# A gated MLP behind linear attention: the spatial product of two of four batches by Strassen's scheme, and another written order

## Chip, cores and metric

One core of one Trainium2 chip runs the whole program. The metric is device time in microseconds (us) of one execution, lower is better. TensorE, VectorE, ScalarE, GpSimd and the queue of SyncE, which issues the DMAs, each run their own list of instructions in the order in which the program wrote them, and wait for one another by semaphores. In rows and code they are PE, DVE, ACT, POOL and SP; PEld is the load of TensorE's stationary operand.

## What is computed

Linear attention with a forget gate comes first, 4 batches of 8 heads, 768 steps, 48 wide; its output, 768 by 384 for each batch, goes into a gated MLP that mixes along the sequence.

```python
f = 1.0 / (1.0 + np.exp(-f_logit))
for t in range(S):
    state = f[:, :, t, :, None] * state + np.einsum('bhd,bhe->bhde', k[:, :, t], v[:, :, t])
    y[:, :, t] = np.einsum('bhd,bhde->bhe', q[:, :, t], state)
...
h = np.maximum(x @ w_in, 0.0)
u, v = (h[..., :d_ff // 2], h[..., d_ff // 2:])
v_n = (v - mu) / np.sqrt(var + 1e-06)
v_s = np.einsum('ts,bsd->btd', w_spatial, v_n) + b_spatial[None, :, None]
gated = u * v_s
return (gated @ w_out)
```

The spatial product is `w_spatial` (768 by 768) times `v_n` (768 by 512), once for each batch.

## The kernel before

**The work is a list of named steps.** `PLAN` (lines 44 to 109) is a table of step names with their arguments; the program calls `step_<name>` for each in turn, and so the table alone sets the order on every engine. A name in `BESIDES` (lines 112 to 119) takes the step's other form: for `sm`, `ys`, `r2` and `c` it says which of two engines does it, for `V`, `U` and `S` it swaps the second and third pass. `Slots` hands out buffers: a step takes one, and it is free again when its last user calls `done`.

**Attention** runs over 24 tiles of 128 tokens (n, six for each batch). The steps `LF`, `LK`, `LQ` load; `c`, `e`, `z`, `h`, `g`, `k`, `q` make the decayed keys and queries; `X`, `YS`, `kv`, `Yq` are its small matmuls in two PSUM pairs `bp`; `w`, `m`, `r0`, `r1`, `r2` stand between them; `ys`, `xt`, `xh`, `xl` copy, transpose and split the tile's output.

**Every large product is done in three passes.** A factor x is held as hi, a copy rounded to the matmul's own type (fp32r), and lo = x - hi; the product is hi·hi + hi·lo + lo·hi, so each 128 by 128 block costs three matmuls. For each of `v`, the gated value and the weights, ScalarE makes hi and VectorE lo.

**The MLP** of batch b, in halves th of 384 tokens:
- `V:b,u` (line 493) makes the v half of h for tile u, 9 matmuls of 512 columns; `vr` is its ReLU, `bs` the moments, `na`, `nb`, `nc` the factor of the norm, `vn` applies it, `vh` and `vl` (lines 562 to 576) split it.
- `U:b,th,c` (line 578) makes u for the block c of 128 channels, 9 matmuls of 384 columns; `ur` is its ReLU.
- `S:b,th,c` (line 592) is the spatial product for 128 channels c and 384 tokens th: 3 passes by 6 blocks of the 768 steps, 18 matmuls of 384 columns in one PSUM bank `mm`. There are 8 such groups for each batch. `sg` (line 606, VectorE) adds the bias and takes the result out of PSUM.
- `sm` multiplies with u, on VectorE or on GpSimd, `sh` and `sl` split, `O:b,th,tt` (line 644) is the output product, 12 matmuls, `oc` copies out and `od` stores.

```python
acc = mm.take(("s", b, th, c))
...
nc.tensor.matmul(
    acc[:, 0:TH], vns.of((b, ks))[va][:, cs], w_sp_s[wb][:, ks, th * TH:(th + 1) * TH],
```

**Buffers.** PSUM has four single banks `mm` and two pairs `bp`. The attention's tiles lie in a pool `attn` on one side of SBUF until the plan ends. At the end of the plan a branch asks whether any gate was too small (`flag`, `check`, `load`), and the last three stores stand behind it.

**The order around the change.** The plan mixes attention and MLP: attention's last tile, `Yq:23`, stands behind all eight `S` of batch 2, and the eight `S` of batch 3 come after attention.

Of the kernel before, what the change touches and what calls it, by code (L numbers as in the profile page):

```python
# [19 lines left out]
T = 128  # L20
# [29 lines left out]
    g:5 LF:7 ct:U,0 c:7 fm:3 w:4 r0:3 m:4 r1:3 r2:3 vr:0,1 xt:2 xh:2 xl:2 ch:U,0 V:0,0 LU:1 YS:4 cl:U,0 LF:6 kv:4  # L50
    h:5 fm:5 fm:4 r0:4 e:7 Yq:3 V:0,2 ys:3 xt:3 LK:5 LQ:5 c:6 e:6 z:6 ca:U,1 r1:4 r2:4 vr:0,0 q:5 LK:6 k:5 ct:U,1
    X:5 g:6 h:6 Yq:4 q:6 U:0,0,0 LF:8 LK:7 vr:0,2 m:5 ys:4 xt:4 nm:0,0 ch:U,1 xh:3 z:7 k:6 c:8 w:5 YS:5 kv:5 cl:U,1
    r1:5 xl:3 X:6 xh:4 xl:4 r0:5 Yq:5 vc:0,1 ys:5 vc:0,2 sq:0,2 h:7 fm:7 q:7 w:6 m:6 g:7 k:7 V:0,3 LQ:6 YS:6 kv:6
    r0:6 e:8 z:8 sq:0,1 vc:0,0 sq:0,0 X:7 w:7 na:0,0 ur:0,0,0 nb:0,0 LF:9 c:9 Yq:6 kj r1:6 xt:5 xh:5 r2:6 m:7 V:0,4
# [36 lines left out]
    sm:2,0,3 g:21 k:21 S:2,1,0 ys:19 od:1,1,0 e:22 xt:19 xh:19 z:22 xl:19 w:20 LF:23 S:2,1,2 YS:20 sg:2,1,0 X:21
# [56 lines left out]
def tile_kernel(ctx, tc, fkq, fn, vv, w_cv, w_spT, b_sp, out):  # L148
# [695 lines left out]
```

## Time and profile before

| | us |
|---|---|
| median of 3 runs | 352.7 (350.92 to 355.41) |
| the profiled execution, its own time | 352.25 |
| its span, first to last instruction | 350.4 |
| outside the span | 1.85 |
| TensorE busy in the span | 334.1 (95%) |
| mean granted TensorE clock | 0.990 of full |

TensorE's busy time counts a matmul until its end leaves the array, so neighbours overlap; what a group of matmuls costs in a run is read from the pieces of the chain of waits, which go from start to start. VectorE's instructions overlap in the same way, by less.

### The profile page before, as it was taken

To read this page: it belongs to the slowest core of one execution; us is meant where nothing else is said; L and a number is where in the kernel's file an instruction comes from. 1 tells how busy PE (TensorE), PEld (TensorE's weight loads), DVE (VectorE), ACT (ScalarE), POOL (GpSimd) and SP (SyncE) were. 2 spreads that over 40 slices of the span, in tenths; PEclk is the share of its full clock that TensorE was granted. 3 is DMA by queue.
4 is the path that set the end of the run, shared out by engine and by line. 5 is a ranking of instruction groups with operands and counts; after the bars stand their busy time and mean duration, and the time that the engine had idled before them with its cause. 6 is when DMAs were issued, how large, how long until landed. Compare 5 with 4: busy or idle time off the path is not lost.

```text
span 350.4 us, 10471 instructions
## 1 busy us (share of the span) xinstructions
PE 334.1 (95%) x4590; PEld 311.7 (89%) x4590; DVE 218.7 (62%) x436; ACT 171.4 (49%) x349; POOL 46.4 (13%) x69
## 2 busy tenths in 40 slices
PE   4689999999999999999999999999999999999993
PEld 3577888989999899999889989999989989999993
DVE  2799879999896966446574675535557657132140
ACT  7776799683645645124544754233443534121231
POOL 3123111303200101003020030012001200001100
PEclk9899999999999999999999999999999999999998
DMA  7849485745323503021630332400101000001012
GB/s 246 331 116 296 153 291 167 281 145 160 91 93 116 204 1 137 2 74 64 178 118 2 125 106 87 159 2 1 47 4 45 4 22 24 22 7 40 23 49 74
DMA packets 14981, 36.01 MB, mean 103 GB/s; under 512 B 1488, under 2 KB 10192, under 8 KB 14928
## 3 DMA queue, kind: packets, MB, share of 16 engines
q1 hardware_dynamic: 14928, 35.26, 30.3%
q8 instruction: 38, 0.62, 0.8%
q14 instruction: 15, 0.12, 0.1%
HBM read 30.54 MB, written 4.72 MB: 101 GB/s over the span
## 4 chain that ended last, share of the span: by engine, by line
PE 89%; DMA 4%; ACT 2%; DVE 1%; issue 1%; SPq 1%; POOL 0%; ACTq 0%; DVEq 0%
PE mm L598 29%; PE mm L636 15%; PE mm L499 14%; PE mm L584 13%; PE bp L385 5%; PE bp L437 4%; PE bp L449 3%; PE bp L409 2%; PE mm L462 2%; DMA fkq<-fkq 2%; DMA words<-w_cv 2%; PE mm L340 2%; POOL fkq L325 0%; DVE fkq L357 0%; SPq L311 0%
## 5 line engine op out<-in xcount | busy, mean ns | idle before, releaser
L607 DVE TENSOR_TENSOR gt<-mm,b_bc 128x384 f32<-128x384 f32 x32 | 17.7, 553 | 37.7 <-PE mm L598 37.7
L598 PE MATMUL mm<-w_sph,vnh 128*128 128x384 f32 x192 | 40.1, 344 | 0.5 <-ACT vr L513 0.5
L598 PE MATMUL mm<-w_spl,vnh 128*128 128x384 f32 x192 | 39.0, 338 | 0.0
L598 PE MATMUL mm<-w_sph,vnl 128*128 128x384 f32 x192 | 39.0, 338 | 0.0
L598 PEld LDWEIGHTS mm<-w_sph,vnh 128*128 128x128 f32 x192 | 33.4, 188 | 0.9 <-ACT vr L513 0.6
L598 PEld LDWEIGHTS mm<-w_spl,vnh 128*128 128x128 f32 x192 | 34.2, 188 | 0.0
L598 PEld LDWEIGHTS mm<-w_sph,vnl 128*128 128x128 f32 x192 | 34.2, 188 | 0.0
L614 POOL TENSOR_TENSOR uT<-gt,uT 128x384 f32<-128x384 f32 x12 | 14.1, 1176 | 149.0 <-DVE gt L607 97.7
L589 ACT ACTIVATE uT<-mm 128x384 f32<-128x384 f32 x32 | 15.5, 489 | 27.4 <-PE mm L584 27.4
L618 ACT CAST gh<-uT 128x384 fp32r<-128x384 f32 x32 | 16.0, 511 | 21.1 <-DVE uT L614 13.4
L622 DVE TENSOR_TENSOR gl<-uT,gh 128x384 fp32r<-128x384 f32 x32 | 17.4, 555 | 13.0 <-ACT gh L618 13.0
L385 PE MATMUL bp<-q,fkq 48*64 48x112 f32 x768 | 23.4, 260 | 0.4 <-DVE fkq L357 0.4
L325 POOL TENSOR_SCALAR fkq<-fkq 112x512 f32<-112x512 f32 (+1 forms) x11 | 16.7, 1515 | 53.4 <-DMA fkq<-fkq 21.7
L584 PE MATMUL mm<-xTh,w_inh 128*128 128x384 f32 x96 | 23.0, 347 | 0.0
L652 ACT COPY osb<-mm 128x384 f32<-128x384 f32 (+1 forms) x25 | 11.4, 465 | 23.6 <-PE mm L636 23.6
L361 DVE TENSOR_TENSOR q<-fkq,F 112x512 f32<-112x512 f32 x24 | 16.4, 684 | 9.6 <-ACT F L346 7.9
L636 PE MATMUL mm<-w_outh,gh 128*128 128x384 f32 (+1 forms) x100 | 22.3, 337 | 0.0
L636 PE MATMUL mm<-w_outh,gl 128*128 128x384 f32 (+1 forms) x100 | 22.1, 333 | 0.0
L584 PE MATMUL mm<-xTh,w_inl 128*128 128x384 f32 x96 | 22.1, 338 | 0.0
L584 PE MATMUL mm<-xTl,w_inh 128*128 128x384 f32 x96 | 22.0, 338 | 0.0
L499 PE MATMUL mm<-w_inh,xTh 128*128 128x512 f32 x72 | 21.8, 410 | 0.0
L636 PE MATMUL mm<-w_outl,gh 128*128 128x384 f32 (+1 forms) x100 | 21.6, 331 | 0.0
(106 smaller groups left out, 704.0 us busy)
## 6 DMA issues: line engine op xcount, KB each, us to landing
fkq<-fkq SPq DMA_DIRECT2D x16, 768.0 KB, 4.6
val<-vv SPq DMA_DIRECT2D x24, 192.0 KB, 4.4
out<-osb SPq DMA_DIRECT2D x24, 192.0 KB, 2.0
fkq<-fkq SPq DMA_DIRECT2D x8, 512.0 KB, 6.0
words<-w_cv SPq DMA_DIRECT2D x4, 768.0 KB, 6.6
fkq<-fn SPq DMA_DIRECT2D x8, 192.0 KB, 3.2
late<-w_cv SPq DMA_DIRECT2D x2, 768.0 KB, 5.7
spat<-w_spT SPq DMA_DIRECT2D x3, 384.0 KB, 5.0
```

Of the source, the lines that this page charges most:

```text
L325: (nc.gpsimd if beside("c", n) else nc.vector).tensor_scalar(f, f, -LOGIT_MOST, None, op0=ALU.max)
L361: nc.vector.tensor_tensor(qs[n % 2][:, :, :, 0:C], *(x.rearrange("p (j c t) -> p j c t", c=T // C, t=C) for x in (parts(n)[2], Fs[n % 2])) ...
L385: nc.tensor.matmul(sc[to, e, cs], k[dr, at:at + C], qs[n % 2][dr, j, chunk], start=True, stop=True)
L499: nc.tensor.matmul(acc, xs[:, c, ut * P:(ut + 1) * P], ws[:, c, G:FF], start=i == 0, stop=i == 3 * KX - 1)
L584: nc.tensor.matmul(acc[:, 0:TH], ws[:, kx, cs], xs[:, kx, :], start=i == 0, stop=i == 3 * KX - 1)
L589: nc.scalar.activation(uTs.take((b, th, c)), mm.of(("u", b, th, c))[:, 0:TH], AF.Relu)
L598: nc.tensor.matmul(acc[:, 0:TH], vns.of((b, ks))[va][:, cs], w_sp_s[wb][:, ks, th * TH:(th + 1) * TH], start=i == 0, stop=i == 3 * KS - 1,)
L607: nc.vector.tensor_tensor(gts.take((b, th, c)), mm.of(("s", b, th, c))[:, 0:TH], b_bc[:, th * TH:(th + 1) * TH], op=ALU.add)
L614: (nc.vector if beside("sm", b, th, c) else nc.gpsimd).tensor_tensor(uT, gts.of((b, th, c)), uT, op=ALU.mult)
L618: nc.scalar.copy(gs.take((b, th, c), HU)[0], uTs.of((b, th, c)))
L622: nc.vector.tensor_tensor(lo, uTs.of((b, th, c)), hi.bitcast(F32), op=ALU.subtract)
L636: nc.tensor.matmul(acc[:, ms], gs.of((b, th, c))[ga][:, ts], w_out_s[wb][:, c, ms], start=c == cs[0] == 0 and ga == wb == 0, stop=c == cs[ ...
```

## The change

Batches 0 and 1 keep the product as it was. For batches 2 and 3 each factor is cut in four, the steps s and the tokens in halves of 384, the channels in halves of 256, and the four block results come from seven block products in place of eight.

- `P:b,k,i` is block product i (1 to 7) for the half k of its 256 channels: 3 passes by 3 blocks, 9 matmuls of 384 columns. A batch has 14 of them. It accumulates in a bank named A, B, D or E; 3, 6 and 7 go on in a bank that has been read out in between.
- `p1`, `p2`, `p3`, `p5`, `c1`, `c3`, `c4`, `c5` are VectorE's additions out of PSUM: 16 for each batch where there were 8 `sg`.
- `xs` makes one of four sums of blocks of v (VectorE, 128 by 384), `ah` and `al` split it: 8 of each for a batch. `vh` and `vl` of the first three tiles are done for 256 of the 512 columns.
- `LY`, `ts`, `th`, `tl`, once: four quarters of the weights are loaded anew, 576 KB each, subtracted (`ts`, VectorE, 128 by 1152) and split into four twin factors (`th` ScalarE, `tl` VectorE). They lie where attention's tiles were; twin 4 takes the place of a quarter of the weights.
- `mst` closes attention's pool and the two PSUM pairs and opens four more single banks, `mn`; `mwin` opens the buffers of the sums, two more `gt` and one more `g`. `mr0` and `mr1` make two tiles of 3 by 512 for v of batches 2 and 3.
- The plan is written anew from the first line to the last: attention ends before the first spatial product of batch 2, `Oa` is not used any more, and `sm`, `c`, `r2` are shared out differently: GpSimd does 13, 8 and 13 of them, where it did 12, 11 and 10.

```diff
 PLAN = """
-    LF:0 constants LF:1 LK:0 kq:0 LF:2 c:0 LQ:0 e:0 kz z:0 kq:1 c:1 e:1 c:2 h:0 q:0 g:0 k:0 LV:1 ca:V,1 ct:V,1 z:1
+    LF:0 constants kz LF:1 kq:1 c:0 e:0 LF:2 kq:0 c:1 LK:0 e:1 z:0 g:0 k:0 h:0 q:0 c:2 kj e:2 LV:1 z:1 LQ:0 ca:V,1
...
-    mm = Slots(tiles(ps, "mm", 4, [P, 512]))
-    bp = Slots(tiles(ps, "bp", 2, [P, 2, 512]))
+    banks = tiles(ps, "mm", 4, [P, 512])
+    mm, bp = Slots(banks), Slots(tiles(pair_pool.enter_context(tc.tile_pool(name="pairs", bufs=1, space=PSUM)), "bp", 2, [P, 2, 512]))
...
+    def step_mst():
+        attn_pool.close()
+        win = win_pool.enter_context(tc.tile_pool(name="win", bufs=1, side="right", reuse_waits="tile"))
+        for i in (1, 2, 3):
+            twin[i] = [win.tile([P, HU, TH], F32R, name=f"T{k}{i}") for k in "hl"]
+        twin[4] = [w[:, 0:HU, TH:S] for w in w_sp_s]
+        made = made_pool.enter_context(tc.tile_pool(name="made", bufs=1, side="right", reuse_waits="tile"))
+        spare.extend(tiles(made, "y", 4, [P, HU, TH]))
+        pair_pool.close()
+        mm.free.extend(tiles(bank_pool.enter_context(tc.tile_pool(name="more", bufs=1, space=PSUM)), "mn", 4, [P, 512]))
+
+    def step_mwin():
+        nonlocal sxs
+        made_pool.close()
+        win = sums_pool.enter_context(tc.tile_pool(name="xsum", bufs=1, side="right", reuse_waits="tile"))
+        sxs = Slots([tuple(win.tile([P, HU, P], F32R, name=f"x{k}{i}") for k in "hl") for i in range(4)])
+        gts.free.extend(tiles(win, "gx", 2, [P, TH]))
+        gs.free.append(tuple(win.tile([P, TH], F32R, name=f"gy{k}") for k in "hl"))
...
-        nc.scalar.activation(vns.take((b, u), 2 * KG)[0], vrs.of((b, u)), AF.Copy, **scaled)
+        cs, uses = direct(b, u), 2 * KG if b not in WIN else 2 if u < HU else 4
+        nc.scalar.activation(vns.take((b, u), uses)[0][:, cs], raw(b, u)[:, cs], AF.Copy, **scaled)
...
+    def step_LY(i):
+        ks, th = {1: (0, 0), 2: (HU, 1), 3: (0, 1), 4: (HU, 0)}[i]
+        src = w_spT[ks * P:(ks + HU) * P, th * TH:(th + 1) * TH]
+        nc.sync.dma_start(spare[i - 1], src.rearrange("(k p) n -> p k n", k=HU))
+
+    def step_ts(i):
+
+        left, right = {1: (3, 1), 3: (2, 3), 2: (2, 1), 4: (4, 2)}[i]
+        nc.vector.tensor_tensor(spare[i - 1], spare[left - 1], spare[right - 1], op=ALU.subtract)
+
+    def step_th(i):
+        nc.scalar.copy(twin[i][0], spare[i - 1])
+
+    def step_tl(i):
+        hi, lo = twin[i]
+        nc.vector.tensor_tensor(lo, spare[i - 1], hi.bitcast(F32), op=ALU.subtract)
+
+    def quarter(b, k, i, j):
+        return raws.of((b, j))[:, :, i * 2 * P + k * P:i * 2 * P + (k + 1) * P]
+
+    SUMS = {1: ((1, 1), (1, 0), (1, 1), ALU.add), 3: ((1, 0), (0, 0), (1, 0), ALU.subtract),
+            2: ((0, 0), (1, 1), (0, 0), ALU.subtract), 4: ((0, 1), (0, 1), (0, 0), ALU.subtract)}
+
+    def step_xs(b, k, i):
+
+        *at, op = SUMS[i]
+        to, x, y = (quarter(b, k, *ij) for ij in at)
+        nc.vector.tensor_tensor(to, x, y, op=op)
+
+    def step_ah(b, k, i):
+        nc.scalar.copy(sxs.take((b, k, i))[0], quarter(b, k, *SUMS[i][0]))
+
+    def step_al(b, k, i):
+        hi, lo = sxs.of((b, k, i))
+        nc.vector.tensor_tensor(lo, quarter(b, k, *SUMS[i][0]), hi.bitcast(F32), op=ALU.subtract)
+        raws.done((b, SUMS[i][0][1]))
...
+    FACTORS = {1: ("A", (0, 0), (0, 0)), 2: ("B", (0, 1), (1, 0)), 3: ("D", 4, (1, 1)), 4: ("E", (1, 1), 4),
+               5: ("D", 1, 1), 6: ("A", 2, 2), 7: ("A", 3, 3)}
+    BANKS = {"A": 4, "B": 1, "D": 2, "E": 1}
+
+    def step_P(b, k, i):
+        name, left, right = FACTORS[i]
+        user = ("P", name, b, k)
+        if i in (1, 2, 4, 5):
+            mm.take(user, BANKS[name])
+        for n, (va, wb) in enumerate(order("P", b, k, i)):
+            for ks in range(HU):
...
+                nc.tensor.matmul(
+                    mm.of(user)[:, 0:TH], x, y, start=n == ks == 0 and i not in (3, 6, 7), stop=n == ks == 2,
+                    skip_group_check=True,
+                )
...
+    def part(name, b, k, th, c, first):
+        acc, at = mm.of(("P", name, b, k))[:, 0:TH], (b, th, c)
+        add = b_bc[:, th * TH:(th + 1) * TH] if first else gts.of(at)
+        nc.vector.tensor_tensor(gts.take(at) if first else add, acc, add, op=ALU.add)
+        mm.done(("P", name, b, k))
+
+    def step_p1(b, k):
+        part("A", b, k, 0, k, True)
...
+    def step_c1(b, k):
+        part("B", b, k, 0, k, False)
```

Three places where the lists of instructions differ.

TensorE, the spatial product of batch 2 before: the last matmul of one group of 18 (`S:2,0,0`) and the first seven of the next. The bank is mm, vnh and vnl are the two parts of v, w_sph and w_spl those of the weights, and the numbers tell buffers apart.

```order
L598 MATMUL mm_130<-w_sph,vnl_154 128x384
L598 MATMUL mm_133<-w_sph,vnh_149 128x384
L598 MATMUL mm_133<-w_sph,vnh_147 128x384
L598 MATMUL mm_133<-w_sph,vnh_145 128x384
L598 MATMUL mm_133<-w_sph,vnh_151 128x384
L598 MATMUL mm_133<-w_sph,vnh_155 128x384
L598 MATMUL mm_133<-w_sph,vnh_153 128x384
L598 MATMUL mm_133<-w_sph,vnl_150 128x384
```

The same batch in the changed kernel: the end of product 4, which has twin 4 for its weights, and products 6, 6 and 7 (Th and Tl are a twin's parts, xh and xl those of a sum of blocks of v).

```order
L733 MATMUL mm_132<-w_sph,vnl_158 128x384
L733 MATMUL mm_133<-Th_3363,xh_3505 128x384 x3
L733 MATMUL mm_133<-Tl_3364,xh_3505 128x384 x3
L733 MATMUL mm_133<-Th_3363,xl_3506 128x384 x3
L733 MATMUL mm_134<-Th_3363,xh_3507 128x384 x3
L733 MATMUL mm_134<-Th_3363,xl_3508 128x384 x3
L733 MATMUL mm_134<-Tl_3364,xh_3507 128x384 x3
L733 MATMUL mm_133<-Th_3365,xh_3511 128x384 x3
```

A pass has three blocks in place of six, and the two halves k=1 and k=0 follow one another in two banks.

VectorE, the list behind the last split of batch 2's v, before: bias additions (L607, gt<-mm) stand among the steps of attention tile 21.

```order
L575 TENSOR_TENSOR vnl_152<-vr_142,vnh_151 128x512
L395 TENSOR_TENSOR sc_117<-bp_135,mask 128x512
L607 TENSOR_TENSOR gt_1344<-mm_130,b_bc 128x384
L325 TENSOR_SCALAR fkq_112<-fkq_112 112x512
L335 SCALAR_TENSOR_TENSOR fkq_112<-runs,fkq_112 112x512
L607 TENSOR_TENSOR gt_1346<-mm_133,b_bc 128x384
```

The same place in the changed kernel: `ts` (L683) and `tl` (L690) on the reloaded quarters y, between additions out of PSUM (L746); twin 4's lo part is written into w_spl.

```order
L702 TENSOR_TENSOR vr<-vr,late 128x3x128
L683 TENSOR_TENSOR y_3370<-y_3372,y_3370 128x1152
L746 TENSOR_TENSOR gt_1296<-mn_3378,gt_1296 128x384
L746 TENSOR_TENSOR gt_1294<-mm_134,b_bc 128x384
L690 TENSOR_TENSOR Tl_3362<-y_3370,Th_3361 128x1152
L746 TENSOR_TENSOR gt_1294<-mm_132,gt_1294 128x384
L683 TENSOR_TENSOR y_3372<-y_3371,y_3372 128x1152
L683 TENSOR_TENSOR y_3371<-y_3371,y_3370 128x1152
L683 TENSOR_TENSOR y_3373<-y_3373,y_3371 128x1152
L690 TENSOR_TENSOR Tl_3364<-y_3371,Th_3363 128x1152
L690 TENSOR_TENSOR Tl_3366<-y_3372,Th_3365 128x1152
L690 TENSOR_TENSOR w_spl<-y_3373,w_sph 128x3x384
```

No step of attention is left here; eight long instructions on the weights have come in.

ScalarE, the start of the program before: the gate of the third tile (fkq_114, L329 and L330) stands behind a step on weights that have to be loaded (L261, words).

```order
L346 ACTIVATE F_121<-mm_130 112x512
L351 ACTIVATE fkq_112<-mm_130 112x512
L261 ACTIVATE words_157<-words_157 128x768
L346 ACTIVATE F_122<-mm_131 112x512
L329 ACTIVATE fkq_114<-fkq_114 128x384
L330 ACTIVATE fkq_114<-fkq_114 128x384
```

And now:

```order
L393 ACTIVATE fkq_112<-mm_131 112x512
L388 ACTIVATE F_121<-mm_131 112x512
L371 ACTIVATE fkq_114<-fkq_114 128x384
L372 ACTIVATE fkq_114<-fkq_114 128x384
L303 ACTIVATE words_159<-words_159 128x768
L433 COPY W_119<-bp_138 128x384
```

The third tile's gate has gone ahead of the weights.

## Rows read from the trace of the kernel before

**Rows 1.** The page: busy time, share of the span and instructions of each engine.

```profile
PE 334.1 (95%) x4590; PEld 311.7 (89%) x4590; DVE 218.7 (62%) x436; ACT 171.4 (49%) x349; POOL 46.4 (13%) x69
```

**Rows 2.** The page: the chain that ended last, by engine.

```profile
PE 89%; DMA 4%; ACT 2%; DVE 1%; issue 1%; SPq 1%; POOL 0%; ACTq 0%; DVEq 0%
```

**Rows 3.** Windows: stretch, length, busy us (count) of PE, PEld, DVE, ACT, POOL, clock.

```profile
0.00:20.00 20.00, 11.65 (x247) 9.78 (x251) 11.38 (x21) 14.69 (x26) 5.13 (x16) 0.91 0.78 273
...
60.00:100.00 40.00, 39.54 (x591) 36.81 (x591) 36.87 (x74) 24.34 (x47) 10.35 (x14) 1.00 0.55 178
...
250.00:270.00 20.00, 19.97 (x338) 18.03 (x337) 12.33 (x27) 8.63 (x18) 1.38 (x3) 1.00 0.06 15
...
310.00:330.00 20.00, 20.00 (x115) 20.00 (x114) 5.21 (x10) 2.80 (x6) 1.37 (x2) 1.00 0.06 20
330.00:351.00 21.00, 14.76 (x93) 14.45 (x91) 4.28 (x8) 5.58 (x13) 0.84 (x1) 0.91 0.18 61
```

**Rows 4.** The chain in order of time: start us, length us, what (matmuls).

```profile
47.12 2.30 PE mm L499 x9
...
88.67 2.09 PE mm L499 x9
...
138.43 9.51 PE mm L598 x54
...
215.84 4.75 PE mm L584 x27
...
291.88 6.29 PE mm L636 x36
```

**Rows 5.** Groups by form on VectorE: count, busy us, mean ns, idle before, releaser.

```profile
L607 DVE TENSOR_TENSOR gt<-mm,b_bc 128x384 f32<-128x384 f32 x32 | 17.7, 553 | 37.7 <-PE mm L598 37.7
L622 DVE TENSOR_TENSOR gl<-uT,gh 128x384 fp32r<-128x384 f32 x32 | 17.4, 555 | 13.0 <-ACT gh L618 13.0
L395 DVE TENSOR_TENSOR sc<-bp,mask 128x512 f32<-128x512 f32 x24 | 16.4, 683 | 4.5 <-PE bp L385 4.4
L575 DVE TENSOR_TENSOR vnl<-vr,vnh 128x512 fp32r<-128x512 f32 x21 | 14.4, 704 | 3.8 <-ACT vnh L565 3.8
L519 DVE BATCH_NORM_STATS2 six<-vr 128x6 f32<-128x512 f32 x21 | 14.3, 681 | 2.9 <-ACT vr L513 2.9
L558 DVE TENSOR_SCALAR vr<-vr,mv,rs 128x512 f32<-128x512 f32 x21 | 11.5, 577 | 0.3
L520 DVE BATCH_NORM_AGGREGATE mv<-six 128x2 f32<-128x6 f32 x21 | 3.8, 182 | 0.7
L428 DVE TENSOR_TENSOR sA<-sA,F 112x192 f32<-112x192 f32 x10 | 3.5, 349 | 0.1
L297 DVE TENSOR_TENSOR w_spl<-late,w_sph 128x768 fp32r<-128x768 f32 x3 | 2.9, 950 | 0.1
```

**Rows 6.** Timeline at the first spatial product: start, length, instruction, [idle before <-releaser].

```profile
72.83 1.32 PE L598 MATMUL mm<-w_sph,vnh 128*128 128x384 f32 x6 [0.46 <-ACT vr L513]
...
73.28 1.29 DVE L575 TENSOR_TENSOR vnl<-vr,vnh 128x512 fp32r<-128x512 f32 x2
74.48 1.22 DVE L335 TENSOR_TENSOR_SCAN fkq<-runs,fkq 112x512 f32<-112x512 f32 x1
```

**Rows 7.** Timeline of the start, ScalarE and TensorE.

```profile
10.20 0.93 ACT L261 ACTIVATE words<-words 128x768 f32<-128x768 f32 x1 [2.17 <-DMA words<-w_cv]
...
11.48 0.54 ACT L329 ACTIVATE fkq<-fkq 128x384 f32<-128x384 f32 x1
...
12.63 1.97 PE L340 MATMUL mm<-tri,fkq 128*64 128x128 f32 x16 [2.40 <-ACT fkq L330]
```

**Rows 8.** The page's DMA issues: count, KB each, median us from issue to landing.

```profile
words<-w_cv SPq DMA_DIRECT2D x4, 768.0 KB, 6.6
...
spat<-w_spT SPq DMA_DIRECT2D x3, 384.0 KB, 5.0
```

**Rows 9.** Timeline: the last matmul.

```profile
344.48 0.28 PE L636 MATMUL mm<-w_outh,gl 128*128 128x192 f32 x1
```

More of the change, by code (lines that the diff above doesn't have):

```diff
@@ L50 @@
[L50 to L54, printed above, removed]
@@ L183, in tile_kernel @@
     sB = tiles(attn, "sB", 2, [DP, J * D])
[L184 to L187 removed]
+    late_tile = const.tile([P, 3 * WB], I32, name="late")
+    vr_tile = const.tile([P, HU, G], F32, name="vr")
+    banks = tiles(ps, "mm", 4, [P, 512])
+    mm, bp = Slots(banks), Slots(tiles(pair_pool.enter_context(tc.tile_pool(name="pairs", bufs=1, space=PSUM)), "bp", 2, [P, 2, 512]))
+    ysbs, raws = Slots([const.tile([P, HD], F32, name="ysb")]), Slots([])
     xTs = Slots([tuple(const.tile([P, KX, TH], F32R, name=f"xT{k}{i}") for k in "hl") for i in range(3)])
[L189 removed]
+    vrs = Slots([vr_tile[:, i] for i in range(HU)])
     vns = Slots([tuple(const.tile([P, G], F32R, name=f"vn{k}{i}") for k in "hl") for i in range(6)])
@@ L192, in tile_kernel @@
     spat = Slots(tiles(stage, "spat", 2, [P, 2, TH]))
-    late = Slots(tiles(const, "late", 1, [P, 3 * WB], I32))
+    late = Slots([late_tile])
     uTs = Slots(tiles(const, "uT", 4, [P, TH]))
-    gs = gts = osbs = None
+    gs = gts = osbs = sxs = None
+    twin, spare = {}, []
     def open_moe(pool):
@@ L217, in constants, with step_mr1, step_mr0 @@
         nc.vector.memset(rescale, -21.5 * math.log(2.0))
+    def step_mr1():
+        whole = late.take("mr1")[:, :].bitcast(F32)
+        raws.free.append(whole[:, 0:HU * G].rearrange("p (u n) -> p u n", n=G))
+        ysbs.free.extend(whole[:, HU * G + i * HD:HU * G + (i + 1) * HD] for i in range(2))
+    def step_mr0():
+        for i in range(HU):
+            vrs.take(("all", i))
+        raws.free.append(vr_tile)
+    def step_mst():
[15 more added lines that the diff above has]
+        gs.free.append(tuple(win.tile([P, TH], F32R, name=f"gy{k}") for k in "hl"))
     def step_kz():
@@ L508, in mean, with raw, direct @@
         return moments[(0 if b == "b" else 2 * b + th) % 3]
+    def raw(b, u):
+        if b not in WIN:
+            return vrs.of((b, u))
+        th, ut = divmod(u, HU)
+        if (b, th) not in raws.held:
+            raws.take((b, th), 4)
+        return raws.of((b, th))[:, ut]
+    def direct(b, u):
+        return slice(0, 2 * P if b in WIN and u < HU else G)
     def step_vr(b, u):
@@ L710, in tile_kernel @@
                 run(what)
-    attn_pool.close()
-    outputs = osbs
+    bank_pool.close()
+    bp = Slots(tiles(ctx.enter_context(tc.tile_pool(name="again", bufs=1, space=PSUM)), "bq", 2, [P, 2, 512]))
+    sums_pool.close()
+    win_pool.close()
+    mm, vrs, outputs = Slots(banks), Slots([vr_tile[:, i] for i in range(HU)]), osbs
     dram = ctx.enter_context(tc.tile_pool(name="dram", bufs=1, space=bass.MemoryType.DRAM))
```

192 lines of the change are left out of this document (118 added, 74 removed).

## The prediction

> **What bounds the kernel now.** I read the page's busy times first: TensorE is busy for 95% of the span, VectorE for 62%, ScalarE for 49%, GpSimd for 13% [rows 1]. The chain of waits says the same from the other end: 89% of the way back from the last instruction is TensorE's own work [rows 2]. The windows show where that isn't so. The first 20 us hold 11.65 us of TensorE work and the last 21 us 14.76; between them TensorE is busy 39.54 of 40, 19.97 of 20 and 20.00 of 20 us [rows 3]. So the middle is worth what its matmuls cost, and a change there gains only if VectorE keeps up. VectorE is dense early (36.87 of 40 us) and falls to 12.33 and 5.21 of 20 late [rows 3]: the room for Strassen's additions is late, and there the change puts them.
>
> The chain gives the price of a matmul in a run: 54 of 384 columns take 9.51 us, 0.176 each; a U of nine takes 4.75/3 = 1.58, an O of twelve 6.29/3 = 2.10, a V of nine 2.09, and 2.30 behind attention's small matmuls [rows 4].
>
> **What TensorE is spared.** Per batch 8 groups of 18 matmuls become 14 of 9: 144 become 126. Over two batches 36 go, 36 x 0.176 = 6.3 us. The shape of a matmul stays, so I take no other price for it. In the new list TensorE comes back from the attention's small matmuls to large ones 19 times in place of 21; at 2.30 - 2.09 = 0.21 each [rows 4] that is 0.4 us. Everything else on TensorE stays in number.
>
> **The start.** TensorE waits 2.40 us for the third tile's gate (L329), which stands behind a weight step that began at 10.20, when its DMA had landed [rows 7]. The new list puts that gate ahead of the weights. At most the 2.40 us are won; but its load and GpSimd's clamp come before it, and the tiles behind it hang on the same short VectorE list, so I take 0.5 won, with ends of 2.4 won and 1.0 lost.
>
> **The first spatial product**, at 72.83 us. TensorE waited 0.46 us here, and VectorE ran with no pause until 74.57, when the last lo of v was done [rows 6]. The new list has eight more short VectorE instructions ahead of that point (four clamps, two r2, one r1, one m) and one copy of about 0.55 less. By the nearest rows, 7 x 0.35 + 0.68 - 0.55 = 2.6 us [rows 5]. The loss lies between 0 (VectorE stood idle for 8.6 of the first 20 us [rows 3], and pauses can be filled; TensorE has one more YS and kv of its own ahead of the point) and 2.6; I take 0.8, nearer to the one wait seen, 0.46.
>
> **The middle.** Attention now ends ahead of the first product of batch 2, so the same VectorE work is done in less time. Before, 92% of the densest stretch left TensorE 39.54 of 40 us [rows 3], and behind the first product the load falls. Cost 0, at worst 1.5.
>
> **The twin stage**, from attention's end to `P:2,1,4`, the first product that needs a twin. TensorE has cover: 4 products at 1.58, 3 U at 1.58, 1 O at 2.10, 3 V at 2.09, in all 19.5 us. VectorE's list up to twin 4's lo:
> - three wide vl at 0.704 and two narrow ones at about 0.41 (a line through 512 and 384 columns, taken to 256), 2.9;
> - two vn at 0.577, 1.2;
> - twelve of the size of L607 or L622 (six xs, four parts, one xl, one ys) at 0.554, 6.6;
> - four ts and four tl of 1152 columns. None is in the trace; 384 columns take 0.555 and 768 take 0.950 [rows 5], so 1152 take 1.35, 10.8 in all.
>
> That is 21.5 us by durations. But in a dense run the next one starts before the last has ended: 73.28 + 1.29 = 74.57, and the next starts at 74.48 [rows 6]; 0.09 us of 27 instructions is 2.4, and 19.1 us remain. So VectorE and TensorE run level here. The end by pitch is 0 lost; by durations 2.0. I take 0.7, for a hand-over or two to ScalarE's `th`. The four reloads hide: a load of 384 KB lands after 5.0 us, one of 768 KB after 6.6 [rows 8], and about 8 us of VectorE's list stand before the first ts. They can start only when attention's last matmuls have left the tiles under them; SyncE's queue has only stores behind them. If that cover were gone, the stage would wait some 5 us.
>
> *The Trainium skill, "VectorE: DVE Perf Modes", in "The DRAIN you can't avoid", holds that the next VectorE operation starts only when the pipe of the last one has emptied, and advises few operations, which speaks against this change. The rows disagree by the 0.09 us above. By that rule the stage goes by full durations: 2.0 lost in place of 0.7, and the total would be 348.6.*
>
> **The product stage**, from `P:2,1,4` to `P:3,0,7`. TensorE: 19 products 30.1, three each of V, U and O 6.3 + 4.7 + 6.3, in all 47.4 us. VectorE: 54 instructions of the size of L607 (13 al, 10 xs, 17 parts, 7 sl, 4 sm, 3 xl) at 0.554 are 29.9; 6 bs at 0.681 + 0.182 are 5.2; 6 vn 3.5; 3 wide and 3 narrow vl 3.3; ten tiny ones at no more than 0.18, 1.8. That is 43.7 us by durations, 92% of TensorE's; by pitch about 37.5, or 79%. It fits either way. One chain is tight: the last V of batch 3, its moments, norm and split (an estimate: 2 bs, 3 vn and 4 vl of rows 5 are 6.3 us, and ScalarE's steps between them some 3), must be done before `P:3,0,4`, with 2 U and 3 O, 9.4 us, of TensorE work in between. I take 0.8 for it, ends 0 and 3. The additions out of PSUM, 16 where there were 8, are within the 43.7; ScalarE and GpSimd have room, with 8.63 and 1.38 busy of 20 us [rows 3]. Four more PSUM banks cost nothing.
>
> **The tail.** The last O, its copy and the three stores behind the branch are as before: the last matmul starts at 344.48 [rows 9] and the span ends at 350.4. `Oa` goes, but an O of 2.10 us stands between the last U and its use. Cost 0, at worst 0.8.
>
> **The sum.** -6.3 - 0.4 - 0.5 + 0.8 + 0.7 + 0.8 = -4.9. The profiled execution took 352.25 us (span 350.4, 1.85 around it), so 347.3. The median of the three runs is 352.7, 0.45 above it; I leave the forecast at 347.3, 1.5% under the median.
>
> **Rivals.**
> - *VectorE becomes the bound of both late stages, by its hand-overs to ScalarE.* Each lo has to wait for its hi. L622 had 13.0 us of idle for 32 instructions before it, 0.41 each [rows 5]. If none of it is hidden, the twin stage has 9 such pairs: 21.5 + 3.7 = 25.2 against 19.5, 5.7 lost; the product stage 26: 43.7 + 10.7 = 54.4 against 47.4, 7.0 lost. Then -6.3 - 0.4 + 0.3 + 12.7 = +6.3, which is 358.5, slower than before. It decides from the point where the waits in the two stages pass 6.4 us. For it: the list behind attention is dense. Against it: the idle before L622 lies mostly in the thin tail, where nothing else was listed; here the list puts other work between hi and lo. Chance 0.10.
> - *VectorE takes full durations*: 2.0 lost in the twin stage, the rest as in the sum, -3.6, 348.6. For it: nothing in the sum allows for a wait on a load. Against it: rows 6 show the overlap. Chance 0.20. *This is the page's rule, as a mechanism of this kernel.*
> - *The start keeps all it gains and VectorE has enough pauses to fill*: -6.3 - 0.4 - 2.4 = -9.1, 343.1. For it: the 2.40 us wait is a single row with one cause. Against it: the first product 60 us later hangs on VectorE's sum, which takes back what TensorE wins ahead of it. Chance 0.17.
> - *The product changes nothing*, because the matmuls weren't the bound: excluded by 20.00 of 20 busy [rows 3] to all but 0.03 (352).
>
> **How the numbers follow.** The forecast has 0.50. With its own ends (stalls 0 to 4 in all, start 1 either way) it reaches from 345 to 350.5. For 8 in 10 the range takes in most of the case of 343.1 and part of that of 358.5: 344 to 352.5. About 2% is what a measurement of this kernel can tell from no change, 7 us here, so 345.6 is the line for faster: the case of the good start, 0.17, mostly, and a small part of the forecast, in all 0.22. Slower by over 2% would be above 359.8: 0.04 out of the hand-over case. The rest, 0.74, lies within 2%.
>
> **What would show it.** Right: 36 fewer matmuls of 128 by 384, nine of a product in 1.58 us; TensorE busy near 328 us; no wait over 1 us before `P:2,1,4`; VectorE over 85% busy for 20 us behind attention, and near 250 us in all. Wrong: TensorE waiting for tl (L690) or al (L709) for several us; the clock below full in the late stages; the first spatial product later than 76 us; a product's matmul slower than 0.176.

## The result, and the profile after

The changed kernel takes 343.39 us (median of 4 runs, 342.36 to 343.81), the kernel before 352.48 beside it (350.92 to 355.41): ratio 0.9728, 95% interval 0.9661 to 0.9796: 9.1 us faster by the medians, 2.7% by the ratio. That is 0.6 us under the low end of the predicted range. The profiled execution took 343.65 us with a span of 341.9, so 8.6 and 8.5 us less than the one of before.

The page of the kernel after, busy times and the chain by engine (they answer to [rows 1, 2]):

```profile
PE 327.2 (96%) x4554; PEld 304.7 (89%) x4554; DVE 251.3 (74%) x491; ACT 181.9 (53%) x369; POOL 48.2 (14%) x70
...
PE 93%; DMA 2%; issue 1%; DVE 1%; ACT 1%; SPq 0%; DVEq 0%
```

There are 36 matmuls fewer, 6.9 us less TensorE work and 33 us more on VectorE, and the chain is TensorE's to 93%. The windows (columns as in [rows 3]):

```profile
0.00:20.00 20.00, 10.75 (x272) 8.95 (x272) 11.49 (x22) 14.14 (x25) 4.56 (x15) 1.00 0.77 272
...
60.00:100.00 40.00, 40.00 (x562) 36.75 (x561) 36.61 (x73) 25.21 (x49) 8.20 (x9) 1.00 0.41 137
220.00:240.00 20.00, 20.00 (x315) 18.80 (x314) 17.16 (x41) 7.53 (x16) 1.07 (x2) 1.00 0.40 130
240.00:260.00 20.00, 20.00 (x105) 18.41 (x105) 17.93 (x25) 10.31 (x20) 1.48 (x2) 1.00 0.09 31
260.00:280.00 20.00, 20.00 (x111) 18.75 (x110) 16.09 (x43) 6.91 (x18) 0.00 (x0) 1.00 0.00 1
280.00:300.00 20.00, 20.00 (x116) 20.00 (x115) 16.08 (x32) 7.60 (x17) 1.14 (x1) 1.00 0.00 1
```

The twin and product stages, 230 to 300 us, show what the prediction called right: VectorE between 80 and 90% busy and TensorE without a gap. TensorE's waits (us in total, times, longest) confirm it: all of them lie in the first 40 us, and all but the last in the first 25.

```profile
PE mm L382 <- ACT fkq L372: 5.5, 2, 4.9
PE bp L479 <- DVE sc L437: 2.1, 1, 2.1
PE bp L479 <- issue: 2.0, 2, 1.6
PE bp L427 <- DVE q L403: 0.6, 2, 0.5
PE bp L451 <- issue: 0.5, 1, 0.5
```

A block product costs what a piece of the chain says (start, length, what), 3.14/18 = 0.174 for a matmul:

```profile
287.09 3.14 PE mm L733 x18
...
296.53 4.73 PE mn L733 x27
```

**Where the 8.5 us of span are.** The last matmul ends at 338.15 where it ended at 344.76: 6.6 less. From there to the end of the span it is 3.8 us where it was 5.7: 1.9 less. The second number is the surprise, since the prediction had 0 for it. The tail before and after, timelines of ScalarE and of SyncE's queue (start, length, instruction, [idle before]):

```profile
342.11 0.48 ACT L652 COPY osb<-mm 128x384 f32<-128x384 f32 x1 [2.00 <-PE mm L636]
344.19 0.92 ACT L652 COPY osb<-mm 128x384 f32<-128x384 f32 x3 [1.60 <-PE mm L636]
344.69 0.84 SPq L657 DMA_DIRECT2D out<-osb  x2
```

```profile
333.44 0.48 ACT L813 COPY osb<-mm 128x384 f32<-128x384 f32 x1 [1.57 <-PE mm L797]
335.57 0.48 ACT L813 COPY osb<-mm 128x384 f32<-128x384 f32 x1 [1.65 <-PE mm L797]
336.84 0.32 ACT L813 COPY osb<-mn 128x192 f32<-128x192 f32 x1 [0.79 <-PE mn L797]
338.18 0.32 ACT L813 COPY osb<-mn 128x192 f32<-128x192 f32 x1 [1.02 <-PE mn L797]
```

Before, `Oa` has made three quarters of three output products in advance; what is left of them ends within 2.7 us, three copies (one of 384 columns, two of 192, for two output tiles) stand in one row of 0.92 us, and two stores are issued from 344.69 on, at the last matmul's end and behind it. After, the products come whole, a copy every 1.3 to 2.1 us, and one store is left. The last wait of SyncE's queue is for these stores (us in total, times, longest), first before, then after:

```profile
SPq L840 <- DMA out<-osb: 3.2, 2, 2.5
```

```profile
SPq L1007 <- DMA out<-osb: 1.4, 1, 1.4
```

### The profile page after: what moved, and what is told of

The parts are those of the page before. It is cut to its first block, busy times and chain, and to the rows that moved or that the text cites. A ratio compares the mean times of both kernels' runs of the same rounds, so it can differ in the third digit from the quotient of the medians.

```text
span 341.9 us, 10491 instructions
## 1 busy us (share of the span) xinstructions
PE 327.2 (96%) x4554; PEld 304.7 (89%) x4554; DVE 251.3 (74%) x491; ACT 181.9 (53%) x369; POOL 48.2 (14%) x70
## 4 chain that ended last, share of the span: by engine, by line
PE 93%; DMA 2%; issue 1%; DVE 1%; ACT 1%; SPq 0%; DVEq 0%
PE mm L658 15%; PE mm L644 12%; PE mm L542 12%; PE mm L797 10%; PE mm L733 7%; PE mn L733 6%; PE bp L427 6%; PE mn L797 5%; PE bp L479 4%; PE bp L491 4%; PE mn L542 3%; PE mn L644 3%; PE mm L504 3%; PE bp L451 3%; DMA words<-w_cv 2%; PE mm L382 2%
## 5 line engine op out<-in xcount | busy, mean ns | idle before, releaser
L399 DVE SCALAR_TENSOR_TENSOR fkq<-fkq 112x512 f32<-112x512 f32 x24 | 17.2, 718 | 11.4 <-ACT fkq L393 6.9
L427 PEld LDWEIGHTS bp<-q,fkq 48*64 48x64 f32 x768 | 19.0, 133 | 4.7 <-DVE q L403 1.9
L377 DVE TENSOR_TENSOR_SCAN fkq<-runs,fkq 112x512 f32<-112x512 f32 x16 | 20.4, 1274 | 2.8 <-ACT fkq L372 2.8
L479 PE MATMUL bp<-val,sc 64*64 64x48 f32 x768 | 16.6, 220 | 4.1 <-DVE sc L437 2.1
L658 PE MATMUL mm<-w_sph,vnh 128*128 128x384 f32 x96 | 20.2, 345 | 0.0
L658 PE MATMUL mm<-w_sph,vnl 128*128 128x384 f32 x96 | 19.5, 338 | 0.0
L658 PE MATMUL mm<-w_spl,vnh 128*128 128x384 f32 x96 | 19.5, 338 | 0.0
L437 DVE TENSOR_TENSOR sc<-bp,mask 128x512 f32<-128x512 f32 x24 | 16.4, 683 | 3.8 <-PE bp L427 3.7
L658 PEld LDWEIGHTS mm<-w_spl,vnh 128*128 128x128 f32 x96 | 17.1, 188 | 0.0
L658 PEld LDWEIGHTS mm<-w_sph,vnl 128*128 128x128 f32 x96 | 17.1, 188 | 0.0
```

The lines of the kernel that those rows point to most:

```text
L377: return nc.vector.tensor_tensor_scan(f[0:DP], runs, f[0:DP], 0.0, op0=ALU.mult, op1=ALU.add)
L399: nc.vector.scalar_tensor_tensor(k, f, 1.0 / F_LEAST, k, op0=ALU.min, op1=ALU.mult)
L427: nc.tensor.matmul(sc[to, e, cs], k[dr, at:at + C], qs[n % 2][dr, j, chunk], start=True, stop=True)
L437: nc.vector.tensor_tensor(Ss[n % 2].rearrange("p (e j t) -> p e j t", e=2, t=C), scores(n)[:, :, :, 0:C], mask.unsqueeze(1).unsqueeze(1).b ...
L479: nc.tensor.matmul(y[to, e, cs], s[rows, keys[e]], v[rows, hd], start=j == 0, stop=False, skip_group_check=True)
L658: nc.tensor.matmul(acc[:, 0:TH], vns.of((b, ks))[va][:, cs], w_sp_s[wb][:, ks, th * TH:(th + 1) * TH], start=i == 0, stop=i == 3 * KS - 1,)
```

## The experiments

The places at which the profiled executions can be compared, in us, read from their timelines ("late part": from the start of attention's last matmul to the end of the last one; "tail": from there to the end of the span):

| kernel | first spatial product | attention's last matmul | late part | tail |
|---|---|---|---|---|
| before, again | 72.83, 73.22 | 283.80, 284.58 | 60.95, 60.95 | 5.69, 5.24 |
| E1 before, whole O | 72.79 | 283.55 | 65.66 | 3.55 |
| E2 the same, no wait | 73.91 | 284.46 | 60.84 | 3.66 |
| after, again | 74.12, 74.67 | 229.77, 230.23 | 108.37, 108.34 | 3.80, 3.76 |
| E3 after with Oa | 74.47 | 231.47 | 108.82 | 5.28 |
| E4 plain product | 71.91 | 229.09 | 115.39 | 3.52 |
| E5 product 4 twice | 74.61 | 230.67 | 114.59 | 3.82 |
| E6 tl twice | 77.33 | 233.18 | 115.65 | 3.67 |
| E7 al twice | 74.13 | 229.91 | 112.00 | 3.85 |
| E8 late gate | 74.38 | 230.20 | 108.33 | 3.90 |
| E9 early mask | 75.16 | 231.06 | 108.36 | 3.74 |
| E10 clamps on GpSimd | 74.11 | 230.50 | 108.40 | 3.75 |

Where the late part is the same code, it agrees to 0.1 us. Up to attention's end the same code differs by up to 2.4 us (E4 and E3), and E6 stands 1.7 behind that: its TensorE stood for 3.1 us near 20 us and then ran on half the clock up to 27.6. E3, E7 and E9 had half the clock for as long in the first 22 us without falling back so far, so what it costs there stays open. A difference of medians under some 1.5 us is not put down to an edit by itself; E2's 1.5 below is at that edge and rests on the tail in its profile.

**The tail.** First the changed kernel again, and E1.

> The changed kernel once more, beside which the next three kernels stand on the same chip. Both theories of the tail expect 343.4 +- 0.7, its last matmul ending near 338.1 and the span 3.4 to 3.8 us after that.

342.90 (6 runs), ratio to before 0.9752 (0.9714 to 0.9790).

```diff
-    ... O:3,0,2 ... U:3,1,3 sg:3,1,3 ur:3,1,3 sm:3,1,3 Oa:3,1,1 Oa:3,1,2 sh:3,1,3 sl:3,1,3 O:3,1,2 oc:3,1,2 Oa:3,1,0 ... O:3,1,0 oc:3,1,0 O:3,1,1 oc:3,1,1
+    U:3,1,3 O:3,0,2 ... sg:3,1,3 ur:3,1,3 sm:3,1,3 ... sh:3,1,3 sl:3,1,3 O:3,1,2 ... oc:3,1,2 ... O:3,1,0 oc:3,1,0 O:3,1,1 oc:3,1,1
```

> The kernel before with its last four output products whole and in turn, and no Oa. Theory A, the tail is 1.9 us shorter because whole products spread the last three copies and stores, where the splitting bunches them: the last matmul ends where it did within 0.3 (344.8), copies stand 1.3 to 2.1 us apart, only one store is issued behind the last copy, and from the last matmul's end to the end of the span it is 3.8 us in place of 5.7; the time falls by 1.9, to about 350.6. Theory B, the order has no price and the last store of the profiled execution merely fell together with a 16 KB packet of instructions on one DMA engine (landing 4.18 us after its issue, where others take 2.0): the tail is 3.8 or 5.7 as that packet falls, and the median of the runs moves by less than 0.7. Theory C, the tail costs nothing as predicted: no change within 0.5; if the first whole product has to wait for the last split, up to 0.8 more.

354.78 (12 runs) against 351.77, ratio 1.0095 (1.0063 to 1.0126): slower by 3.0. The tail is as theory A has it, 3.55, but TensorE had to wait for the last splits, and then ran on half the clock. Its timeline, and its windows (length, TensorE busy, granted clock):

```profile
338.79 0.44 PE L636 MATMUL mm<-w_outh,gh 128*128 128x384 f32 x1 [0.93 <-ACT gh L618]
341.05 0.45 PE L636 MATMUL mm<-w_outh,gh 128*128 128x384 f32 x1 [1.83 <-ACT gh L618]
341.34 1.30 PE L636 MATMUL mm<-w_outl,gh 128*128 128x384 f32 x4
```

```profile
339.00:341.00 2.00, 0.22 (x1) 1.00 0.28 102
341.00:343.00 2.00, 1.95 (x7) 0.63 0.02 4
343.00:345.00 2.00, 2.00 (x8) 0.52 0.03 8
345.00:347.00 2.00, 2.00 (x15) 1.00 0.27 98
```

The waits are 2.8 us, the late part is 4.7 longer: most of the rest is the 3.4 us at half clock. So this is what `Oa` was there for, and E1 doesn't price the tail. E2 takes that wait away with a sixth buffer g in the place of attention's tiles:

```diff
+    def step_gw():
+        attn_pool.close()
+        more = more_pool.enter_context(tc.tile_pool(name="more", bufs=1, side="right", reuse_waits="tile"))
+        gs.free.append(tuple(more.tile([P, TH], F32R, name=f"gy{k}") for k in "hl"))
...
+    U:3,1,1 gw U:3,1,2 ... U:3,1,3 ... O:3,0,0 ... O:3,0,2 ... O:3,1,2 ... O:3,1,0 oc:3,1,0 O:3,1,1 oc:3,1,1
```

> The kernel before with its last four output products whole, as in the first try, but without that one's wait of 2.8 us: one more buffer g (in the place of attention's tiles) lets the last U stand two output products ahead of its use. Tail theory: the last matmul ends within 0.4 of where it did, the tail is 3.4 to 3.8 us in place of 5.7, the median falls by 1.5 to 2.1 us against the kernel before. Rival, the tail is worth nothing: within 0.5.

350.14 (12 runs) against 351.65, ratio 0.9966 (0.9935 to 0.9996): 1.5 us faster by the medians, 0.1 to 2.3 by the interval. Late part 60.84 as before, tail 3.66 in place of 5.69 or 5.24. The other way round, E3:

```diff
-    O:3,1,2 od:3,0,0 oc:3,1,2 O:3,1,0 O:3,1,1
+    Oa:3,1,1 Oa:3,1,2 O:3,1,2 od:3,0,0 oc:3,1,2 Oa:3,1,0 O:3,1,0 O:3,1,1
```

> The changed kernel with the three Oa steps of the kernel before put back ahead of its last three output products; the matmuls are the same. Theory A (bunched copies and stores): the last three copies start within 1 us of each other, two stores are issued behind the last matmul, the tail grows from 3.4 - 3.8 to about 5.7, the time by 1.9, to 345.3. Theory B (a packet of instructions in the way): tail 3.8 or 5.7 as the packet falls, median within 0.7 of the changed kernel. Theory C: nothing, 343.4.

346.26 (6 runs), ratio 0.9848 (0.9809 to 0.9886), 3.4 us slower than the changed kernel beside it. Tail 5.28 in place of 3.76. Of the rest, 1.2 us lie ahead of attention's end, where the code is the same (a wait of 1.06 for a clamp at 97 us is most of it), 0.5 in the late part. And a second look at the kernel before:

> The kernel before once more, for a second profile of its tail. The tail theory (the split output products bunch the last three stores, so that one delayed store is the last of all) expects again two stores behind the last matmul, the last of them landing 3.5 to 4.2 us after its issue, and 5.3 to 5.7 us from the last matmul's end to the end of the span. The theory of chance expects 3.5 to 5.7.

352.48 (one run), tail 5.24. So with `Oa` the tail was 5.2 to 5.7 in three profiles, without it 3.5 to 3.9 in eleven. How long the stores were under way (from issue to landing, least, median, most) shows how: the last two of E2, and the last two of before in its second profile.

```profile
DMA to landing us min/median/max: 2.2/3.1/3.9
```

```profile
DMA to landing us min/median/max: 2.1/2.9/3.7
```

In the first the slow one is the last but one, in the second it is the last. In all 14 profiles one of the last three stores took 3.2 to 4.2 us where most take about 2.1. Without `Oa` it is the last but one, and hidden; with `Oa` it is the last. In all 14 the trace also has a 16 KB packet of the instruction queue that starts 0.9 to 1.3 us behind the issue of the slow store. So theory A is right about the copies, the stores and the tail; the packet of theory B may be what slows the store. No run moves that packet by itself, so that it is the cause is not shown, and neither is whether bunching the stores or shifting them against the packet makes the end wait.

**The product.** E4 keeps the new order and takes the scheme out, E5 puts the spared matmuls back.

```diff
-    P:2,1,1 ... P:2,0,1 ... xs:2,1,1 ... ts:1 ... th:1 ... tl:1 ... P:3,1,3 ... c3:3,1
+    S:2,0,1 ... sg:2,0,1 ... S:2,0,0 ... S:2,1,0 ... sg:2,1,0 ... S:3,0,0 ... S:3,1,1 ... sg:3,1,1
```

> The changed kernel's order and buffers with the plain spatial product in both late batches: 8 groups of 18 matmuls each in place of 14 of 9, no sums, twins or reloads, and nothing left out of the result. Theory 1, the seven products are worth their 36 matmuls and nothing else, since VectorE's additions lie beside TensorE's work: 342.9 + 6.3 = 349.2 +- 0.8, with the tail of the changed kernel (3.4 to 3.8 us). Theory 2, the additions cost TensorE about 2 us of waits, as the prediction had it: 347.2. Theory 3, the new order alone brings nothing but the tail: 352 - 1.9 = 350.1, which is within theory 1's range and can't be told from it.

350.68 (12 runs), ratio 0.9976 (0.9956 to 0.9997). Its late part is 7.0 longer than the changed kernel's 108.35; 0.6 of that is a wait that only this list has (a V that waits for a split on ScalarE). That leaves 6.4 for 36 matmuls: theory 1, though the median lies 0.7 above its range, most of it by that wait. The order alone is worth 0.8 us by the ratio, less than the 1.7 to 2.2 by which its tail is shorter (3.52 against 5.24 and 5.69): the rest of the new order brings nothing that shows.

```diff
+    def step_P0(b, k, i):
+        step_P(b, k, i, True)
-    P:2,1,4 ... P:2,0,4 ... P:3,0,4 ... P:3,1,4
+    P0:2,1,4 P:2,1,4 ... P0:2,0,4 P:2,0,4 ... P0:3,0,4 P:3,0,4 ... P0:3,1,4 P:3,1,4
```

> The changed kernel with product 4 made twice in each of the four half batches (its bank is written anew the second time): 36 more matmuls of 128 by 384, as many as the change spares, and nothing more on VectorE. Theory 1, the late stages are bound by TensorE alone: 36 x 0.176 = 6.3 us more, 349.7 +- 0.7. Theory 2, VectorE's additions bound them in part and TensorE has hidden slack: 2 to 4 us more.

350.13 (10 runs), ratio 0.9962 (0.9932 to 0.9992). The late part grows by 6.2, 0.173 for each matmul: TensorE alone bounds it.

**VectorE's room.** E6 and E7 do each split of one kind twice; the second time writes the same values again.

```diff
-    tl:1 ... tl:2 ... tl:3 ... tl:4
+    tl:1 tl:1 ... tl:2 tl:2 ... tl:3 tl:3 ... tl:4 tl:4
```

> The changed kernel with each of the four splits of a twin (tl, 128 by 1152 on VectorE, 1.28 us from one to the next) done twice: 5.1 us more on VectorE ahead of product 4 of batch 2. In the changed kernel the lo part of twin 4 ends at 250.01 and the first matmul that reads it starts at 250.06. Theory 1, the two engines run level to within a tenth of a us in the twin stage and TensorE has no slack behind it: product 4 waits about 5 us on tl (L690), TensorE's busy time stays, the time is 348.3 +- 0.7. Theory 2, VectorE has room there, as its 80 to 90 per cent of busy time suggests: less than 2 us more.

350.89 (10 runs), ratio 0.9983 (0.9958 to 1.0008). TensorE's waits and its clock in the stretch:

```profile
PE mm L733 <- DVE w_spl L690: 5.2, 1, 5.2
```

```profile
254.00:256.00 2.00, 0.00 (x0) 1.00 0.00 0
256.00:258.00 2.00, 0.00 (x0) 0.57 0.00 0
258.00:260.00 2.00, 0.96 (x3) 0.50 0.00 0
260.00:262.00 2.00, 2.00 (x8) 0.50 0.00 0
262.00:264.00 2.00, 2.00 (x10) 0.73 0.00 0
```

Theory 1, and 1.9 more than its range allowed: 5.1 us added, 5.2 waited, 7.3 lost in the late part, since the clock fell to half while TensorE stood and stayed there for the next 4 us of matmuls.

```diff
-    al:2,1,2 ... al:3,1,4
+    al:2,1,2 al2:2,1,2 ... al:3,1,4 al2:3,1,4
```

> The changed kernel with each of the 16 splits of a sum (al, 128 by 384 on VectorE) done twice: 16 x 0.47 = 7.5 us more on VectorE, 10 of the 16 between product 4 of batch 2 and the last product of batch 3's first half. Theory 1, VectorE has room in the product stage (it is idle for 9.9 us between 240 and 300 us): 0.5 to 1.5 us more, and that in the first products behind twin 4, where VectorE is dense. Theory 2, VectorE's durations bound this stage as well (43.7 of 47.4 by the prediction's durations, so 52.6 with the doubles): 5 us more, spread over both batches. Theory 3, the hand-overs from ScalarE's split to VectorE's count 0.41 each: 8 us or more.

347.50 (10 runs), ratio 0.9901 (0.9856 to 0.9945). The late part grows by 3.65 of the 7.5 added, between theories 1 and 2. Of that, 2.6 comes within 8 us behind twin 4, where TensorE waits for VectorE to read out a bank that goes on with product 7 (first row) and for splits (second):

```profile
PE mm L736 <- DVE gt L749: 1.4, 1, 1.4
PE mm L736 <- DVE xl L709: 0.5, 2, 0.3
```

**The start.**

```diff
-    e:2 LV:1 z:1 LQ:0 ca:V,1 ct:V,1 X:0
+    LV:1 z:1 LQ:0 ca:V,1 ct:V,1 e:2 X:0
```

> The changed kernel with the third tile's gate behind the weight step on ScalarE, as in the kernel before; nothing else differs. Theory 1, the start's gain is given back by the first spatial product: TensorE waits about 2.4 us for that gate again near 10 us, but the first spatial product stands at 74.1 +- 0.5 and the time at 343.4 +- 0.7. Theory 2, the change's early gate is worth its wait: 345.8. A fall of the granted clock in the first 20 us, as in the profile of the kernel before (0.50 from 12.7 to 16.1), may add to either.

342.70 (4 runs), ratio 0.9748 (0.9720 to 0.9777). Theory 1: the third tile's gate is late by 2.5 us, the first spatial product stands at 74.38, the time is that of the changed kernel.

```diff
-    ca:V,1 ct:V,1 X:0 w:0 h:1 g:1 LK:1 z:2 ch:V,1 m:0 k:1 YS:0
+    ca:V,1 X:0 w:0 m:0 ct:V,1 h:1 g:1 LK:1 z:2 ch:V,1 k:1 YS:0
```

> The changed kernel with the first tile's mask step on VectorE (m:0) ahead of the three shift steps of the weights (ct:V,1) in place of behind them; the first score product moves up with it. In the changed kernel the first value product waited 2.1 us for m:0. Theory 1, the first spatial product hangs on VectorE's sum up to it, and what TensorE wins in the first 20 us is given back by then: the value product starts 1.5 to 2 us earlier, the first spatial product stays at 74.1 +- 0.5, and the time at 343.4 +- 0.7. Theory 2, TensorE's early wait is a loss that is carried to the end: 341.5.

344.66 (6 runs), ratio 0.9803 (0.9765 to 0.9841). The first tile's value product (`YS:0`) starts at 12.10 in place of 13.37, and the next score product (`X:1`) waits 2.62 for VectorE, which now does the weights first. Theory 2 falls; theory 1 is right that nothing is won, but the first spatial product (75.16) and the time each come 0.6 later than it allowed. In this profile the granted clock was 0.50 from about 15 to 22 us, which may have a part in it.

```diff
 BESIDES = """
+    c:5 c:7 c:8 r2:3 r2:6
```

> The changed kernel with three clamps (c:5, c:7, c:8) and two state steps (r2:3, r2:6) on GpSimd in place of VectorE, as the kernel before had them: 1.9 us less on VectorE ahead of the first spatial product. Theory 1, that product hangs on VectorE's sum: it stands 1 to 1.9 us earlier than 74.1 + the start's 0 to 1 us, and the time falls by as much, to about 341.5. Theory 2, other chains bind (a clamp takes 1.5 us on GpSimd in place of 0.4, a state step 0.7 to 0.9 in place of 0.36): no gain, 342.9 to 344.

343.56 (6 runs), ratio 0.9772 (0.9739 to 0.9805). With 1.9 us less on VectorE the first spatial product stands where it stood, at 74.11: theory 2.

## Why the prediction was wrong, step by step

**TensorE is spared 6.3 us:** right, 6.2 (E5) and 6.4 (E4). The 0.4 for two returns fewer from attention's small matmuls was isolated by no run.

**The start, 0.5 won, and the first spatial product, 0.8 lost:** the sum of +0.3 was about right, judged by what the other terms leave over; the reasons weren't. The third gate is early as foreseen, but the next wait is right behind it (compare [rows 7]; TensorE's timeline after):

```profile
10.20 1.09 PE L382 MATMUL mm<-tri,fkq 128*64 128x128 f32 x16
13.37 0.68 PE L479 MATMUL bp<-val,sc 64*64 64x48 f32 x32 [2.08 <-DVE sc L437]
13.87 0.54 PE L451 MATMUL bp<-val,W 64*48 64x48 f32 x32
```

E8 gives the gate back at no cost: the start is worth 0. The first spatial product stands 1.3 later in the first profiles, and 1.4 by the middle values of the four profiles with the old start (72.79 to 73.91) and the seven with the new one (71.91 to 77.33), which spread too far to fix the size. About 1.0 of it would be TensorE's own additional YS and kv (0.50 and 0.54, as in these rows), work that is only moved ahead of the point; this is argued, not tried. The 0.8 was built on VectorE's sum. E10 takes 1.9 us from it and nothing moves, though its steps are slower on GpSimd; and TensorE has no pause in the 34 us ahead of the point (windows after, columns as in [rows 3]), so that there it hangs on TensorE's own list:

```profile
40.00:60.00 20.00, 20.00 (x485) 17.84 (x486) 17.45 (x35) 18.59 (x41) 0.38 (x2) 1.00 0.77 267
60.00:74.00 14.00, 14.00 (x275) 11.87 (x273) 13.28 (x30) 10.15 (x20) 2.99 (x3) 1.00 0.45 157
```

**The middle, 0:** right, TensorE is busy 40.00 of the 40 us from 60 to 100.

**The twin stage, 0.7 lost:** it cost 0.06. "VectorE and TensorE run level here" was right to a hair. VectorE's last step of the stage and the first matmul that reads it:

```profile
242.07 4.12 DVE L683 TENSOR_TENSOR y<-y,y 128x1152 f32<-128x1152 f32 x3
246.12 2.62 DVE L690 TENSOR_TENSOR Tl<-y,Th 128x1152 fp32r<-128x1152 f32 x2
248.66 1.35 DVE L690 TENSOR_TENSOR w_spl<-y,w_sph 128x1152 fp32r<-128x1152 f32 x1
```

```profile
249.47 0.70 PE L733 MATMUL mm<-w_sph,vnh 128*128 128x384 f32 x3
250.06 0.80 PE L733 MATMUL mm<-w_spl,vnh 128*128 128x384 f32 x3
```

The lo part of twin 4 is done at 250.01, its first reader starts at 250.06, and E6 shows that every us more is paid, with the clock on top. The 27 instructions took 21.3 us with 1.0 of idle, nearer to the durations' end (21.5) than to 19.1. But VectorE began them at 228.73, 1.2 us ahead of the first block product, and the first three matmuls of `P:2,1,4` (0.6 us) don't need the lo part; the sum had counted neither. These errors cancelled, which was luck. *The Trainium skill, "VectorE: DVE Perf Modes", in "The DRAIN you can't avoid", has the next operation wait until the pipe of the last one is empty, and adds that one that is not held starts earlier; the prediction took the first half alone. The rows show both: the three ts, each of which needs a quarter that its neighbour reads or writes, take 4.12 us, three times their 1.35 and a little more; the two tl stand 2.54/2 = 1.27 apart, less than their 1.35. That the shared quarters make the difference is argued from these rows alone.*

**The product stage, 0.8 lost:** it cost 0. The tight chain was not tight: the last lo of v that `P:3,0,4` needs ends at 283.23 and is read at 284.81. E7 shows about half of 7.5 us as room.

**The tail, 0, at worst 0.8 lost:** this is the step that failed most. "The last O, its copy and the three stores behind the branch are as before" looked at the last matmul alone. Between its end and the end of the span lay 5.7 us [rows 9], of which no row was asked for; that `Oa` goes was weighed for the wait it hides, not for the three copies and two stores it bunches. What the runs show in its place: the tail is 5.2 to 5.7 us with `Oa` and 3.5 to 3.9 without, worth 1.5 (E2's medians, E3's tail) to 1.9 (the first profiles).

With 0 for both stages and -1.9 for the tail the sum would have been -8.3, and 343.95; the profiled execution measured -8.6. The range needed both errors to fail: with the tail alone put right the sum gives 345.45, with the 1.5 of the two stages alone 345.85, and both lie inside 344 to 352.5.

**The rivals.** The hand-overs as the bound: no. Where the list is dense they all but vanish (VectorE's groups after; the last column is idle before, in all, and its releaser):

```profile
L783 DVE TENSOR_TENSOR gl<-uT,gh 128x384 fp32r<-128x384 f32 x29 | 16.1, 560 | 0.1
L709 DVE TENSOR_TENSOR xl<-vr,xh 128x384 fp32r<-128x384 f32 x8 | 4.4, 552 | 2.5 <-ACT xh L705 2.5
L709 DVE TENSOR_TENSOR xl<-late,xh 128x384 fp32r<-128x384 f32 x8 | 4.3, 551 | 0.0
```

Of the 2.5, 2.3 lie behind 300 us. The 13.0 us of idle in the row of 32 in [rows 5] were mostly the thin tail's, as argued against it: 6.1 lie behind 300 us, 3.0 between 280 and 300, and 3.9 ahead of that. Full durations: VectorE's list came near them (21.3 of 21.5), but no time was lost by it. The good start named the time nearly (343.1), by luck: no stalls, yes, but the 2.4 us of the start were given back and the tail took their place.

## What to carry to other kernels

Read the last microseconds like a stage of their own: the last matmul's end, each copy, each store from issue to landing, and what the end waits for. A trick that hides a wait of the last product by splitting several (`Oa`) makes them all end together, and here it paid with the stores; one more buffer hid the same wait at no cost in time. And before a dense stage is called free, ask how much it would take to break it: here 0.05 us in one place and 4 in the next.

## What was not expected of the hardware

- A wait of TensorE in a full stretch can cost more than itself: 5.2 us became 7.3 (E6), and with two waits of 2.8 us together the late part grew by 4.7 (E1), since the granted clock went to 0.50 (1.2 GHz) and stayed there for the next 4 and 3.4 us of matmuls. It need not: waits of 1.4 us (E7, near 256 us) and 1.06 us (E3, near 97 us) left the clock at 1.00. *The Trainium skill, "TensorE: Matmul & The Clock Gate", in "Part 1: The HAM clock gate (the "warmup" mystery)", says that the throttled state is the default and activity releases it; E6's rows agree: the clock fell while TensorE stood and rose again behind matmuls.*
- In the first 30 us the clock differs between executions of the same kernel; in 9 of the 14 profiles it was at 0.50 for a while. Before, first and second profile (12 to 16 us):

```profile
12.00:14.00 2.00, 1.37 (x14) 0.65 1.05 369
14.00:16.00 2.00, 2.00 (x70) 0.50 0.82 326
```

```profile
12.00:14.00 2.00, 1.83 (x16) 1.00 1.02 374
14.00:16.00 2.00, 2.00 (x75) 1.00 0.91 348
```

  The first spatial product came 0.4 us later all the same in the second; what the early clock costs was not isolated.
